# A two-layer GELU block on one core: w1's first four tiles in two transfers, and no half dummies around the transposes

## The chip, the core and the metric

The kernel runs on one core of a Trainium2 chip. The metric is the device time of one execution in microseconds, as the median of several runs. A profile of one execution stands beside it; its "span" goes from the first to the last instruction of the core, and the device time of the same execution is a little longer. In the profile PE is TensorE's matmul, PEld its weight load, DVE is VectorE, ACT ScalarE, POOL GpSimd and SP SyncE; a q behind an engine means its instruction queue.

## The reference

```python
B, S, D, F = 1, 2048, 448, 1792          # all inputs in bfloat16
def reference(x, w1, b1, w2, b2):
    h = jnp.einsum("bsd,df->bsf", x, w1) + b1
    h = _gelu(h)                          # tanh approximation
    return jnp.einsum("bsf,fd->bsd", h, w2) + b2
```

## The kernel before

The 2048 rows of x are worked through in four chunks of 512. For each chunk the first layer computes h transposed: the 1792 columns of w1 are 14 tiles ("ft") of 128, taken as seven pairs. The depth of 448 is three slices of 128 and a rest of 64. Every matmul of the layers uses half the rows of the array (64), so that two run side by side, one on the upper and one on the lower half. A pair of tiles is done in two parts, `a` (one half of the rows of each slice, three steps) and `b` (the other half, three steps and the rest of 64); `Layer1.step` picks the weights and writes down what the matmul waits for: the part of w1 that holds the tile (`w1_of`, by the list `W1CUTS`), the rest `w1r`, and the columns of x. ScalarE applies GELU and the bias b1 from PSUM (L268). The second layer multiplies by w2, VectorE adds b2 (L311), SP stores.

No scheduler decides the order. `Program` keeps one list per engine in the order in which the code appends to it, and turns each named event into a semaphore wait at the consumer. So each engine runs in exactly the order of the text, and a transfer is issued where its queue's list has it.

The opening is what the change concerns. SP issues x's first chunk (L153), then waits for ScalarE's "table" activation (L175, which loads the activation table), and only then issues the rest: w1r's first part, w1's tiles 4 to 7, w1r's second part, w1's tiles 8 to 13, w2 in two parts, b2, and the later chunks of x by transposing transfers (L147). w1's tiles 0 to 3 are issued on ScalarE's queue, right behind the table activation (`load_w1(0, "scalar")`). GpSimd makes the identity matrix, zeroes b2_z and fetches b1.

TensorE starts with dummies (`warm`, L191), matmuls of ones by ones into a PSUM tile that later work overwrites: seven of 512 columns and one of 256. `turn_all` then transposes the first chunk of x: twelve transposes of 128x128 (L338, three for each tile t = 0 to 3), whose results VectorE (t = 0, 2) and ScalarE (t = 1, 3) copy from PSUM to xT (L345), then two transposes of the rest xr (L359), which VectorE and ScalarE copy in two pieces each (L368). Then comes one more dummy of 256 columns. On VectorE's list there follow `turn_b1`, four small transposes (L180) and a cast (L182) of b1, and two copies of the odd tiles of w1r from rows 64 to 127 into rows 0 to 63 (L382). The first of them is what the last step of the first pair needs on rows 0 to 63 ("w1rU").

The first layer of chunk 0 begins with the first two pairs, `L[0]` (tiles 0 and 1) and `L[1]` (tiles 2 and 3), in halves of 256 rows of x: `L[0].a` and `L[1].a` on the first 256 rows, which need t = 0 and 1 alone, then both on the second 256. Then come `L[0].b`, `L[2].a` (tiles 4 and 5), `L[1].b`, and from there on one `a` and one `b` by turns.

Of the kernel before, what the change touches and what calls it, by code (L numbers as in the profile page):

```python
# [73 lines left out]
def bass_standalone__dense_activation_gelu__prompt_kernel(  # L74
# [13 lines left out]
    HC = SC // 2  # L88
# [9 lines left out]
    with ExitStack() as es:  # L98
# [21 lines left out]
        ones_m = one.broadcast_to([P, SC])  # L120


        W1CUTS = (0, 4, 8, 14)

        def w1_of(ft):
            return max(i for i, c in enumerate(W1CUTS) if c <= ft)

        def load_w1(i, engine="sync"):
            c0, c1 = W1CUTS[i] * P, W1CUTS[i + 1] * P
            pr.dma(engine, lambda e: e.dma_start(  # L130
                w1_sb[:, :, c0:c1], w1[0:D3, c0:c1].rearrange("(k p) f -> p k f", p=P)), ("w1", i))
# [3 lines left out]
        def load_w1r(i, engine="sync"):  # L135
            cs = slice(RCUTS[i] * P, RCUTS[i + 1] * P)
            pr.dma(engine, lambda e: e.dma_start(w1r[H:P, cs], w1[D3:D, cs]), ("w1r", i))

        def load_w2(a, b):
            pr.dma("sync", lambda e: e.dma_start(  # L140
                w2_sb[:, a:b, :], w2[a * P:b * P, :].rearrange("(f p) d -> p f d", p=P)), ("w2", a))
# [11 lines left out]
        pr.dma("sync", lambda e: e.dma_start(xn[:, :, :], x0v), "x")  # L153
        pr.barrier("sync", ["table"])
        load_w1r(0)
        load_w1(1)
        load_w1r(1)
        load_w1(2)
        load_w2(0, 7)
        load_w2(7, 14)  # L160
        pr.dma("sync", lambda e: e.dma_start(b2_bc[:, :], b2.partition_broadcast(P)), "b2")
# [12 lines left out]
               after=["b1z"])  # L174
        pr.op("scalar", lambda e: e.activation(junk[:, :], one, ACT.Gelu_apprx_tanh), event="table")  # L175
        load_w1(0, "scalar")

        def turn_b1():
            for q in range(4):
                pr.op("vector", lambda e, q=q: e.transpose(  # L180
                    b1t[32 * q:32 * q + 32, :], b1n[:, 32 * q:32 * q + 32]), after=["b1n"], event=("b1t", q))
            pr.op("vector", lambda e: e.tensor_copy(b1_f[:, :], b1t[:, 0:NFT]),  # L182
                  after=[("b1t", q) for q in range(4)], event="b1")
# [5 lines left out]
        def warm(n, cols=SC):  # L189
            for _ in range(n):  # L190
                pr.op("tensor", lambda e: e.matmul(unit[0][:, 0, 0:cols], lhsT=ones_w, rhs=ones_m[:, 0:cols],  # L191
                                                   start=True, stop=True))
# [156 lines left out]
        def turn_all():  # L349


            pr.op("vector", lambda e: e.tensor_copy(  # L352
                xr[:, :, :].rearrange("p q (two h) -> p q two h", two=2),
                xn[:, :, D3:D].rearrange("p (q two) h -> p q two h", two=2)), after=["x"], event="xr_in")
            for t in range(STC):
                turn(t)
                evac(("vector", "scalar")[t % 2], t)
            for q in range(STC // 2):
                pr.op("tensor", lambda e, q=q: e.transpose(  # L359
                    stage(0)[:, q * P:(q + 1) * P], xr[:, q, :], ident[:, :]),  # L360
                    after=["xr_in", ("xT0", 0)], event=("xr", q))
            halves = (slice(0, H), slice(H, P))
            for src, engine in enumerate(("vector", "scalar")):
                i = stage(0)[halves[src], 0:2 * P].rearrange("p (q s) -> p q s", q=2)
                for dst in (src, 1 - src):
                    o = xT[halves[dst], KT, 0:SC].rearrange("p (q two s) -> p q two s", q=2, two=2)[:, :, src, :]
                    pr.op(engine, lambda e, o=o, i=i, engine=engine:
                          e.copy(o, i) if engine == "scalar" else e.tensor_copy(o, i),  # L368
                          after=[("xr", 0), ("xr", 1)], event=("xR0", dst, src))
            busy[(3, 0)] = ("xR0", 1, 0)  # L370
            busy[(3, 2)] = ("xR0", 0, 1)

        warm(NWARM)
        warm(1, HC)
        turn_all()
        warm(1, HC)
        turn_b1()

        for i in (0, 1):
# [78 lines left out]
```

## Time and profile before

| what | value |
|---|---|
| device time, median of 5 runs | 94.38 us (94.03 to 94.87) |
| device time of the profiled execution | 94.03 us |
| its span | 92.7 us |
| PE busy | 89.7 us, 97% of the span |
| ACT busy | 38.4 us, 41% |
| DVE busy | 13.4 us, 14% |
| PE, dummies (L191) | 9 instructions, 3.6 us busy |
| PE, transposes (L338, L359) | 12 from 4.04 us and 2 from 5.03 us |
| PE, first matmul of the layers (L216) | 5.34 us after the span's start |
| x, first chunk: 448 KB on SP's queue | 3.2 us from issue to landing |
| w1, tiles 0 to 3: 384 KB on ACT's queue | 4.4 us from issue to landing |

Busy times may overlap, since a matmul that is streaming and one that drains both count. Idle time on an engine that isn't the bound costs nothing; a wait is charged to the thing that came last before the waiting engine went on.

### The profile page before, as it was taken

The page shows a single profiled execution, that of the slowest core. Times are in us where ns is not written, and L with a number is a line of the kernel's source. Part 1 is how long each engine was busy: PE and PEld are TensorE (multiplying, and loading weights), DVE is VectorE, ACT ScalarE, POOL GpSimd, SP SyncE. Part 2 cuts the span into 40 slices and gives each one's busy share as a digit, 9 for nine tenths or more (in the row PEclk, how much of TensorE's full clock was granted, in tenths as well). Part 3 has the DMA queues.
Part 4 walks back from the last instruction along what each step waited for, and adds up shares of the span by engine and source line. Part 5 has one row for each costly group of instructions (what it writes and reads, how often), then busy time and mean ns, then how long its engine had stood idle before and what let it go on. Part 6 is the DMA issues. An engine that isn't in the chain of part 4 may idle for free.

```text
span 92.7 us, 2060 instructions
## 1 busy us (share of the span) xinstructions
PE 89.7 (97%) x932; PEld 50.1 (54%) x932; DVE 13.4 (14%) x33; ACT 38.4 (41%) x63; POOL 1.7 (2%) x8
## 2 busy tenths in 40 slices
PE   6999999999999999999999999999999999999990
PEld 2474444665654444556654444565554444576990
DVE  0183001010441000000433000000333000000421
ACT  6065878600005787700003787900002887900001
POOL 6000000000000000000000000000000000000000
PEclk9999999999999999999999999999999999999999
DMA  2999999654658000000033000000022000000022
GB/s 40 358 277 298 361 324 151 111 99 99 77 96 212 21 0 7 0 0 0 0 103 102 0 0 4 0 7 0 0 99 99 0 0 7 0 0 7 33 66 99
DMA packets 12344, 7.32 MB, mean 79 GB/s; under 512 B 6960, under 2 KB 12144, under 8 KB 12336
## 3 DMA queue, kind: packets, MB, share of 16 engines
q1 hardware_dynamic: 11904, 6.80, 31.5%
q10 hardware_dynamic: 400, 0.39, 1.2%
q8 instruction: 7, 0.11, 0.5%
q0 software_dynamic: 32, 0.00, 0.0%
q14 instruction: 1, 0.01, 0.0%
HBM read 3.79 MB, written 1.84 MB: 61 GB/s over the span
## 4 chain that ended last, share of the span: by engine, by line
PE 97%; ACT 0%; issue 0%
PE u L216 92%; PE u L191 4%; PE u L338 1%; ACT out_sb L328 0%; PE u L359 0%
## 5 line engine op out<-in xcount | busy, mean ns | idle before, releaser
L268 ACT ACTIVATE g<-u,b_f 128x512 bf16<-128x512 f32 x56 | 35.0, 684 | 40.0 <-PE u L216 40.0
L216 PE MATMUL u<-w_sb,g 64*128 64x448 bf16 (+1 forms) x504 | 43.9, 328 | 0.0
L216 PE MATMUL u<-xT,w_sb 64*128 64x512 bf16 (+1 forms) x348 | 42.9, 369 | 0.0
L216 PEld LDWEIGHTS u<-w_sb,g 64*128 64x128 bf16 x504 | 28.1, 94 | 14.7
L216 PEld LDWEIGHTS u<-xT,w_sb 64*128 64x128 bf16 x348 | 19.7, 94 | 18.6 <-DMA w_sb<-in_w_dram 0.2
L311 DVE TENSOR_TENSOR out_sb<-u,b_bc 128x448 bf16<-128x448 f32 x14 | 8.1, 620 | 59.8 <-PE u L216 59.8
L216 PE MATMUL u<-xT,w1r 64*128 64x512 bf16 x56 | 16.4, 376 | 0.0
L216 PEld LDWEIGHTS u<-xT,w1r 64*128 64x128 bf16 x56 | 5.3, 94 | 3.6 <-DVE w1r L382 0.4
L191 PE MATMUL u<-const-bfloat16-1.0 128*128 128x512 bf16 (+1 forms) x9 | 3.6, 565 | 0.8 <-PEq L443 0.8
L328 ACT CAST out_sb<-u 128x224 bf16<-128x224 f32 x1 | 0.3, 345 | 9.3 <-PE u L216 9.3
L191 PEld LDWEIGHTS u<-const-bfloat16-1.0 128*128 128x128 bf16 x9 | 1.1, 135 | 2.4 <-issue 2.4
L345 ACT COPY xT<-u 128x384 bf16<-128x384 bf16 x2 | 0.9, 482 | 2.5 <-PE u L338 2.5
L175 ACT ACT_TABLE_LOAD x1 | 1.3, 1283 | 0.7 <-PEq L443 0.7
L186 DVE COPY xT<-xT 64x512 bf16<-64x512 bf16 x3 | 0.9, 289 | 3.6 <-DMA xT<-in_x_dram 3.6
L406 DVE COPY b_z<-b_bc 1x448 bf16<-1x448 bf16 x1 | 0.3, 269 | 6.7 <-DMA b_bc<-in_b_dram 6.7
L338 PEld LDWEIGHTS u<-ident,xn 128*128 128x128 bf16 x12 | 0.8, 108 | 0.6 <-issue 0.6
L338 PE MATMUL u<-ident,xn 128*128 128x128 bf16 x12 | 0.9, 236 | 0.0
L319 DVE TENSOR_TENSOR out_sb<-u,b_bc 128x448 bf16<-128x448 f32 x1 | 0.6, 625 | 1.8 <-PE u L216 1.8
L180 DVE STREAM_TRANSPOSE b1t<-b1n 32x32 bf16<-32x32 bf16 x4 | 0.8, 202 | 0.1
L368 ACT COPY xT<-u 64x256 bf16<-64x256 bf16 x2 | 0.7, 368 | 0.0
L345 DVE COPY xT<-u 128x384 bf16<-128x384 bf16 x2 | 0.7, 358 | 0.4 <-PE u L338 0.4
L352 DVE COPY xr<-xn 128x256 bf16<-128x256 bf16 x1 | 0.2, 228 | 3.0 <-DMA xn<-in_x_dram 3.0
(18 smaller groups left out, 4.8 us busy)
## 6 DMA issues: line engine op xcount, KB each, us to landing
out_dram<-out_sb SPq DMA_DIRECT2D x16, 112.0 KB, 1.7
w_sb<-in_w_dram SPq DMA_DIRECT2D x2, 784.0 KB, 8.5
w_sb<-in_w_dram SPq DMA_DIRECT2D x1, 576.0 KB, 6.3
xn<-in_x_dram SPq DMA_DIRECT2D x1, 448.0 KB, 3.2
w_sb<-in_w_dram ACTq DMA_DIRECT2D x1, 384.0 KB, 4.4
w_sb<-in_w_dram SPq DMA_DIRECT2D x1, 384.0 KB, 4.4
xT<-in_x_dram SPq DMA_TRANSPOSE x12, 4.4
w1r<-in_w_dram SPq DMA_DIRECT2D x1, 160.0 KB, 4.3
```

The lines of the kernel that those rows point to most:

```text
L175: pr.op("scalar", lambda e: e.activation(junk[:, :], one, ACT.Gelu_apprx_tanh), event="table")
L180: pr.op("vector", lambda e, q=q: e.transpose(b1t[32 * q:32 * q + 32, :], b1n[:, 32 * q:32 * q + 32]), after=["b1n"], event=("b1t", q))
L186: pr.op("vector", lambda e: e.tensor_copy(xT[0:H, KT, s0:s1], xT[H:P, KT, s0:s1]), after=after, event=event)
L191: pr.op("tensor", lambda e: e.matmul(unit[0][:, 0, 0:cols], lhsT=ones_w, rhs=ones_m[:, 0:cols], start=True, stop=True))
L216: o = pr.op("tensor", lambda e: e.matmul(unit[u][:, lo, cols], lhsT=lhsT, rhs=rhs, start=start, stop=stop, skip_group_check=skip), after=a ...
L268: pr.op("scalar", lambda e, lo=lo, ft=ft: e.activation(g[:, ft, c * SC:(c + 1) * SC], unit[u][:, lo, :], ACT.Gelu_apprx_tanh, bias=b1_f[:, ...
L311: pr.op("vector", lambda e, lo=lo, j=j: e.tensor_tensor(out=out_sb[:, j, :], in0=unit[u][:, lo, 0:D], in1=b2_bc[:, :], op=ALU.add), after= ...
L319: pr.op("vector", lambda e: e.tensor_tensor(out=out_sb[:, j, :].rearrange("p (two h) -> p two h", two=2), in0=unit[u][:, :, 0:DH], in1=b2_ ...
L328: pr.op("scalar", lambda e: e.copy(out_sb[:, j, DH:D], unit[u][:, 1, 0:DH]), after=[y[1]], event=("o", j, 1))
L338: pr.op("tensor", lambda e, k=k: e.transpose(stage(t)[:, k * P:(k + 1) * P], xn[:, t, k * P:(k + 1) * P], ident[:, :]), after=["ident", "x ...
L345: pr.op(engine, lambda e: e.copy(o, i) if engine == "scalar" else e.tensor_copy(o, i), after=[("xt", t)], event=("xT0", t))
L368: e.copy(o, i) if engine == "scalar" else e.tensor_copy(o, i),
```

## The change

`W1CUTS` gets one more cut, so that w1's tiles 0 and 1 and its tiles 2 and 3 are two transfers with a semaphore each (192 KB each, runs of 512 B instead of 1024 B). Both are issued on ScalarE's queue, one right behind the other. The numbers of SP's two parts of w1 go up by one; their contents and order stay. The half dummy before the transposes and the one after them are taken out. The order on the other engines is the same; on TensorE the first matmul of tiles 2 and 3 now has a wait of its own.

```diff
-        W1CUTS = (0, 4, 8, 14)
+        W1CUTS = (0, 2, 4, 8, 14)
...
         pr.dma("sync", lambda e: e.dma_start(xn[:, :, :], x0v), "x")
         pr.barrier("sync", ["table"])
         load_w1r(0)
-        load_w1(1)
+        load_w1(2)
         load_w1r(1)
-        load_w1(2)
+        load_w1(3)
...
         pr.op("scalar", lambda e: e.activation(junk[:, :], one, ACT.Gelu_apprx_tanh), event="table")
         load_w1(0, "scalar")
+        load_w1(1, "scalar")
...
         warm(NWARM)
-        warm(1, HC)
         turn_all()
-        warm(1, HC)
         turn_b1()
```

## The prediction

> **What bounds the kernel now.** I read the page's shares and its chain first, then the waits of the opening, then the opening in order of time on PE and on DVE, and last the transfers.
>
> The page of the kernel before, its shares and its chain:
>
> ```profile
> PE 89.7 (97%) x932; PEld 50.1 (54%) x932; DVE 13.4 (14%) x33; ACT 38.4 (41%) x63; POOL 1.7 (2%) x8
> ...
> PE 97%; ACT 0%; issue 0%
> PE u L216 92%; PE u L191 4%; PE u L338 1%; ACT out_sb L328 0%; PE u L359 0%
> ```
>
> TensorE is the bound from end to end. The two layers (L216) are 92% of the 92.7 us span, and the change doesn't touch one of their instructions. So it can only move the moment at which the stream of L216 becomes gapless. The dummies (L191) are the 4% at the start. The waits between 3.5 and 9 us say where that moment is set (engine, line, what it waited for; us, times, longest):
>
> ```profile
> PEld u L216 <- DVE w1r L382: 0.4, 1, 0.4
> ...
> PEld u L359 <- DVE xT L345: 0.2, 1, 0.2
> PEld u L216 <- DMA w_sb<-in_w_dram: 0.2, 1, 0.2
> ```
>
> The change addresses the last of these, the wait for w1's first part. The reader should see that it isn't the last wait of the opening: L216 waits again, and longer, for the copy of w1r on VectorE. In order of time (start us, us), PE and then DVE:
>
> ```profile
> 4.04 0.95 PE L338 MATMUL u<-ident,xn 128*128 128x128 bf16 x12
> 5.03 0.27 PE L359 MATMUL u<-ident,xr 128*128 128x128 bf16 x2
> 5.14 0.27 PE L191 MATMUL u<-const-bfloat16-1.0 128*128 128x256 bf16 x1
> 5.34 2.13 PE L216 MATMUL u<-xT,w_sb 64*128 64x256 bf16 x30
> 7.32 0.64 PE L216 MATMUL u<-xT,w1r 64*128 64x512 bf16 x2
> 7.57 1.67 PE L216 MATMUL u<-xT,w_sb 64*128 64x512 bf16 x12
> ```
>
> ```profile
> 3.93 0.23 DVE L352 COPY xr<-xn 128x256 bf16<-128x256 bf16 x1 [3.01 <-DMA xn<-in_x_dram]
> 4.53 0.69 DVE L345 COPY xT<-u 128x384 bf16<-128x384 bf16 x2 [0.37 <-PE u L338]
> 5.42 0.60 DVE L368 COPY xT<-u 64x256 bf16<-64x256 bf16 x2 [0.20 <-PE u L359]
> 6.04 0.90 DVE L180 STREAM_TRANSPOSE b1t<-b1n 32x32 bf16<-32x32 bf16 x4
> 7.08 0.17 DVE L182 CAST b_f<-b1t 128x14 f32<-128x14 bf16 x1
> 7.29 0.22 DVE L382 COPY w1r<-w1r 64x256 bf16<-64x256 bf16 x1
> ```
>
> From 5.42 to 7.51 VectorE has no idle time between its instructions. Its copy at L382 ends at 7.51, and the second w1r matmul of the first pair starts at 7.56. Its partner started at 7.32, so PE loses 7.56 - 7.32 = 0.24 us there. That is the slack: PE may enter L216 up to 0.24 us later, or any amount earlier, and still be at 7.56. What sets 7.56 is the chain x lands (3.91) -> transposes -> copies of x on DVE -> turning b1 -> copy of w1r.
>
> The transfers of the opening (KB, us from issue to landing):
>
> ```profile
> q10 hardware_dynamic: 400, 0.39, 1.2%
> ...
> xn<-in_x_dram SPq DMA_DIRECT2D x1, 448.0 KB, 3.2
> w_sb<-in_w_dram ACTq DMA_DIRECT2D x1, 384.0 KB, 4.4
> w_sb<-in_w_dram SPq DMA_DIRECT2D x1, 384.0 KB, 4.4
> ```
>
> ScalarE's transfer is issued at 0.80 and lands at 0.80 + 4.4 = 5.19. Its packets (queue 10: 384 of 1024 B and 16 completions) run from 3.24 to 4.62 in the trace, beginning only as those of x end (1.77 to 3.50). By the row each takes 1.2% x 92.7 x 16 / 384 = 46 ns.
>
> **The first half dummy goes.** It is 256 columns at the slow clock: 0.21 us of array, from 3.72 to 3.93. x's semaphore completes at 3.91, and the first transpose starts its weight load at 4.01; PE's wait for x is a separate instruction at 3.94, so what remains until 4.01 is the wait's own latency. The dummy was over in time. Worth: 0 (between 0 and -0.1, the time from x's semaphore to the weight load). Afterwards PE stands idle from 3.72 to 4.04, 0.32 us instead of 0.11.
>
> **The second half dummy goes.** At 5.14 it takes 256 columns, 0.11 us at full clock. The first layer's first half needs the tiles t=0 and t=1 of x, and ScalarE's copy of t=1 ends at 5.17; PE passes that wait at 5.26. With w1 there and no dummy, the weight load comes at about 5.29 instead of 5.34: 0.05 us earlier. All of it falls into the slack at 7.56. Worth: 0.
>
> **w1's first four tiles in two transfers.** The bytes stay; runs fall from 1024 to 512 B, so there are 768 packets instead of 384, 24 per DMA engine in each transfer. The second issue takes another 0.45 us of ScalarE's queue (by the first: 0.80 to 1.25), until 1.70. Queued behind it is the copy of t=1 at 4.69, so that is hidden by 3 us; the table load and the activation that SP's barrier waits for (2.24) are dispatched before both. On SP nothing is added; only numbers of w1's parts shift.
>
> When do the halves land? No packet of 512 B from w1 is in the trace. Lower end: half the bytes take half the time, so the first half's packets end 0.69 us earlier and it lands near 4.5, the second at 5.19 as now. Upper end: a 512 B packet takes as long as one of 1024 B; then the first lands at 5.19 and the second 1.39 us later, at 6.58. The Trainium skill (page "DMA: Bandwidth & Descriptors", section "Why small descriptors are slow (HBM only)") counts a packet as its bytes over 32 plus about 3 cycles: 2 x (16 + 3) = 38 cycles where there were 35. By that, 8.6% of 1.39 us, 0.12 us: an estimate, with the second half at about 5.3. The trace's neighbours support the lower half: x's 3584 B packets took 186 ns and w1's 1024 B 46 ns, so time goes by bytes there. I take 4.5 and 5.3. The same page speaks against the split in "Rules for kernel authors" (coalesce small transfers), but 192 KB behind a full x isn't limited by start-up: its packets queue behind x in any case.
>
> Need: the first half at 5.29, satisfied. The second half at 5.29 + 0.34 (the six matmuls of the first pair took 5.34 to 5.68) = 5.63. It lands at 5.3: no stall. Even at 5.87 the 0.24 us of slack would cover it.
>
> What is late next are the transfers queued behind: w1's tiles 4 to 7 land at 2.87 + 4.4 = 7.26 and are first needed at 7.57 (0.31 us in hand), and tiles 8 to 13 land at 4.02 + 6.3 = 10.3, needed near 10.6. Both are moved by the same 0.12 us and both keep 0.2 us.
>
> Sum against the profiled execution (94.03 us, span 92.7): 0 - 0.05 covered, 0.12 of transfers covered, so 94.0. The median of the five is 94.38, and this execution is the fastest.
>
> **The clock of TensorE.** The dummies run one in 0.43 us for 512 columns and the matmuls of 512 columns in the first layer one pair in 0.22, so the dummies are at half the clock. The record of the granted clock starts at 4.33, 3.55 us after the first dummy (0.78). The Trainium skill (page "TensorE: Matmul & The Clock Gate", section "Part 1: The HAM clock gate") says that the clock rises after a busy window of about 3.4 us whose phase is free, so that it varies between executions. The row agrees with a window from 0.91 to 4.33; the rule adds that other executions get the clock later. In such an execution the transposes and both dummies are at half clock, 12 x 0.107 = 1.28 us of transposes end near 5.33, the xr ones near 5.54, and the second dummy's 0.21 us is then on PE's path, because PE rather than VectorE is late. Removing it gives back up to 0.21 us there. The five times (94.03 to 94.87) would fit such a spread, but one trace can't show it. By the row alone the sum is 0; by the rule -0.21 in late executions. I take -0.1 for the median: 94.38 - 0.1 = 94.3.
>
> **The rivals.** *Hidden, as above* (0.60): 94.3, own range 94.0 to 94.7. For it: the wait at L382 behind the wait at w1.
>
> *PE's start counts in most executions* (0.14): if the clock comes late in most of them, the dummy's 0.21 us and some of the wait for w1 are saved: 94.38 - 0.21 - 0.16 = 94.0. Against it: in the only trace PE waits for VectorE afterwards.
>
> *The clock gate misses its window* (0.15), the one on the other side. Place: the idle stretch 3.72 to 4.04, 0.32 of a 3.4 us window, 9% instead of 3%, with short gaps around the xr transposes. If the window has to be busier than that, the clock rises one window later, at 4.33 + 3.41 = 7.74. Half speed for 3.41 us costs 1.7 us of matmuls, less the 0.24 + 0.05 of slack: +1.4 us, 95.8 if every execution misses, 95.1 if half do. It decides as soon as the threshold lies above 91% busy. Against it: a gap of 0.11 us was tolerated in the trace.
>
> *Small packets are slow* (0.11): with the upper end the second half lands at 6.58, PE stalls 0.95 us at tiles 2 and 3, and what follows is moved by up to 1.39 us, so tiles 4 to 7 land at 8.65 instead of 7.26 against a need of 7.57: +1.08 us, 95.5; a third of the way, +0.2. It begins to count when the second half lands after 5.87 or tiles 4 to 7 after 7.57.
>
> **How the numbers follow.** The predicted time is 94.3. About 0.5% (0.47 us) is what a measurement of this kernel can tell from no change. Faster by more, under 93.91, needs the early-start case and luck: 0.09. Slower by more, over 94.85, is most of the clock case and most of the packet case: 0.22. The rest, 0.69, is no change. The range 93.9 to 95.1 holds the hidden case, the early start, the lighter half of both slower ones, and leaves out the full misses.
>
> **What would show it.** Right: PE's L216 starts near 5.29 with no wait on w1, and still resumes near 7.56 after the wait on L382, now longer than 0.36 us; the two ACT transfers land near 4.5 and 5.3; tiles 4 to 7 near 7.4. Wrong: the clock's record starting near 7.7, a wait on w1's second half inside the first 24 matmuls of L216, a wait for tiles 4 to 7 at 7.6, or L382 itself ending earlier than 7.5, which would mean that something moved VectorE's chain that I have left standing.

## The result, and the profile after

The changed kernel takes 94.50 us in the median of 43 runs (93.94 to 94.89); the kernel before took 94.28 us in 80 runs beside it (93.86 to 94.87). The ratio is 1.0024, with a 95% interval of 1.0013 to 1.0036: about 0.23 us slower, where 0.1 us faster was forecast. Ratios leave out executions more than 1.5% above the fastest of their kernel: below, 2 of 11 of the kernel cut by rows, 1 of 22 of the one cut by depth and 7 of 12 of the one with four transfers, and none elsewhere.

The profiled execution of the changed kernel took 94.73 us with a span of 93.4 us, 0.7 us longer than the span before. The page's chain, by engine and by line:

```profile
PE 89%; DMA 6%; ACT 1%; SPq 1%; ACTq 1%; issue 0%; DVE 0%
PE u L217 89%; DMA w_sb<-in_w_dram 6%; SPq L137 1%; ACTq L130 1%; ACT L175 1%; DVE out_sb L326 0%; ACT junk L175 0%
```

Before, the chain was PE from end to end. Now a transfer of w1 stands in it. The waits from 3 to 16 us name it (engine, line, waited for; us, times, longest):

```profile
PEld u L217 <- DMA w_sb<-in_w_dram: 0.7, 1, 0.7
PE u L217 <- DMA w_sb<-in_w_dram: 0.4, 1, 0.4
PEld u L217 <- DVE w1r L381: 0.4, 1, 0.4
```

PE and the weight load wait at the same place, so the first two rows are one stop, not two. PE in order of time (start us, us) shows where it is:

```profile
4.12 0.83 PE L339 MATMUL u<-ident,xn 128*128 128x128 bf16 x12 [0.22 <-DMA xn<-in_x_dram]
4.99 0.27 PE L360 MATMUL u<-ident,xr 128*128 128x128 bf16 x2
5.28 2.13 PE L217 MATMUL u<-xT,w_sb 64*128 64x256 bf16 x30
7.25 0.67 PE L217 MATMUL u<-xT,w1r 64*128 64x512 bf16 x2
8.33 1.04 PE L217 MATMUL u<-xT,w_sb 64*128 64x512 bf16 x8 [0.41 <-DMA w_sb<-in_w_dram]
```

The layers start at 5.28 instead of 5.34, and the pause for VectorE's copy of w1r is where it was (that copy runs from 7.25 to 7.47). But the next matmuls, those of tiles 4 and 5, start at 8.33 where they had started at 7.57. That is 0.76 us, and less the 0.06 us by which the layers start earlier it is the longer span. The transfers on the page (KB, us from issue to landing) say why:

```profile
q10 hardware_dynamic: 800, 0.39, 1.4%
...
w_sb<-in_w_dram SPq DMA_DIRECT2D x1, 576.0 KB, 6.5
xn<-in_x_dram SPq DMA_DIRECT2D x1, 448.0 KB, 3.2
w_sb<-in_w_dram ACTq DMA_DIRECT2D x2, 192.0 KB, 3.9
w_sb<-in_w_dram SPq DMA_DIRECT2D x1, 384.0 KB, 5.4
```

The row of 384 KB is w1's tiles 4 to 7. It is issued at 2.87 as before and lands after 5.4 us instead of 4.4: at 8.28, not 7.26. The two halves on ScalarE's queue land at 4.61 and 5.35, in time.

### The profile page after: what moved, and what is told of

Read it like the earlier page. It is cut to its first block, busy times and chain, and to the rows that moved or that the text cites. A ratio compares the mean times of both kernels' runs of the same rounds, so it can differ in the third digit from the quotient of the medians.

```text
span 93.4 us, 2057 instructions
## 1 busy us (share of the span) xinstructions
PE 89.7 (96%) x930; PEld 46.0 (49%) x930; DVE 13.4 (14%) x33; ACT 38.4 (41%) x63; POOL 1.7 (2%) x8
## 4 chain that ended last, share of the span: by engine, by line
PE 89%; DMA 6%; ACT 1%; SPq 1%; ACTq 1%; issue 0%; DVE 0%
PE u L217 89%; DMA w_sb<-in_w_dram 6%; SPq L137 1%; ACTq L130 1%; ACT L175 1%; DVE out_sb L326 0%; ACT junk L175 0%
## 5 line engine op out<-in xcount | busy, mean ns | idle before, releaser
L217 PE MATMUL u<-w_sb,g 64*128 64x448 bf16 (+1 forms) x504 | 43.2, 328 | 0.0
L217 PE MATMUL u<-xT,w_sb 64*128 64x512 bf16 (+1 forms) x348 | 40.9, 369 | 0.4 <-DMA w_sb<-in_w_dram 0.4
L217 PEld LDWEIGHTS u<-w_sb,g 64*128 64x128 bf16 x504 | 24.5, 94 | 18.4
L217 PEld LDWEIGHTS u<-xT,w_sb 64*128 64x128 bf16 x348 | 16.9, 94 | 19.4 <-DMA w_sb<-in_w_dram 0.7
L217 PE MATMUL u<-xT,w1r 64*128 64x512 bf16 x56 | 10.9, 376 | 0.0
L217 PEld LDWEIGHTS u<-xT,w1r 64*128 64x128 bf16 x56 | 2.8, 94 | 3.7 <-DVE w1r L381 0.4
L192 PE MATMUL u<-const-bfloat16-1.0 128*128 128x512 bf16 x7 | 3.1, 621 | 0.8 <-PEq L442 0.8
L381 DVE COPY w1r<-w1r 64x256 bf16<-64x256 bf16 (+1 forms) x2 | 0.6, 288 | 1.7 <-DMA w1r<-in_w_dram 1.7
```

What stands on the lines that cost most here:

```text
L217: o = pr.op("tensor", lambda e: e.matmul(unit[u][:, lo, cols], lhsT=lhsT, rhs=rhs, start=start, stop=stop, skip_group_check=skip), after=a ...
```

## The experiments

Theory A: the split delays the transfers behind it, and TensorE stops in front of tiles 4 to 7. Theory B, the rival: the half dummies were holding the clock or the pace of the opening, and their loss is what costs. Later, A was divided into A1 (the short runs, twice the packets) and A2 (a second transfer behind the first on ScalarE's queue). Each kernel was timed in five rounds beside the kernel before.

**The split alone** (both half dummies stay; against the changed kernel):

```diff
+        warm(1, HC)
         turn_all()
+        warm(1, HC)
```

> The split alone, both half dummies kept. Theory A (the split delays the transfers behind it, w1's tiles 4 to 7 land at 7.6 or later and TensorE stops in front of them): as slow as the changed kernel, +0.2 to +0.3 us on the kernel before, tiles 4 to 7 landing after 7.6 in the trace. Theory B (the dummies were holding the clock or the pace): no slower than before, -0.1 to 0 us, tiles 4 to 7 landing near 7.3.

Ratio 1.0023 (1.0007 to 1.0039). Tiles 4 to 7 took 5.0 us to land, at 7.87:

```profile
w_sb<-in_w_dram SPq DMA_DIRECT2D x1, 384.0 KB, 5.0
```

In this profiled execution the clock rose late (the twelve transposes take 1.44 us instead of 0.83) and TensorE only came to tile 4 at 8.60, so there was no stop to be seen in it; the time, over 22 runs, is that of the full change. A as forecast, B wrong.

**The dummies alone** (from the kernel before):

```diff
-        warm(1, HC)
         turn_all()
-        warm(1, HC)
```

> The two half dummies taken out, w1's first four tiles in one transfer as before. Theory A: -0.1 to 0 us on the kernel before; first matmul of the layers still near 5.3, held by w1's landing at 5.2. Theory B: +0.2 to +0.3 us.

Ratio 0.9989 (0.9969 to 1.0009), so not slower by more than 0.09 us. Tiles 4 to 7 landed at 2.87 + 4.1 = 7.0:

```profile
w_sb<-in_w_dram SPq DMA_DIRECT2D x1, 384.0 KB, 4.1
```

B is out.

**The need put off, in the kernel before and in the changed one:**

```diff
         L[0].b()
-        L[2].a()
         L[1].b()
+        L[2].a()
```

> The kernel before with L[1].b ahead of L[2].a, so that tiles 4 to 7 are first needed some 0.86 us later (8 matmuls of 512 columns, two side by side, 0.216 us a pair), near 8.4. If the kernel before too waits for tiles 4 to 7 in many executions (its times spread from 93.9 to 94.9), this gives -0.2 to -0.4 us and a narrower spread. If its spread comes from the phase of the clock (theory B's relative), the time stays within 0.1 us and the spread stays.

> The changed kernel with the same order, L[1].b ahead of L[2].a. Theory A: the loss disappears, the time falls to that of the kernel before in the same order, -0.2 to -0.4 us on the kernel before, and no wait for w1 over 0.1 us near 8.4. Theory B: it stays +0.2 us over the kernel before in the same order.

Kernel before: 0.9998 (0.9979 to 1.0017), with the same spread, so it isn't waiting for tiles 4 to 7 as a rule. Changed kernel: 0.9997 (0.9977 to 1.0017), so its loss is gone, though this interval and that of the changed kernel (1.0013 to 1.0036) just touch. Of my two sizes the fall of 0.2 to 0.4 us was a miss; the equality of the two was as A said. PE of the changed kernel in this order:

```profile
7.28 0.66 PE L217 MATMUL u<-xT,w1r 64*128 64x512 bf16 x2
7.56 1.03 PE L217 MATMUL u<-xT,w_sb 64*128 64x512 bf16 x6
8.22 0.59 PE L217 MATMUL u<-xT,w1r 64*128 64x512 bf16 x2
8.43 0.81 PE L217 MATMUL u<-xT,w_sb 64*128 64x512 bf16 x5
```

Tiles 4 to 7 landed at 2.87 + 4.9 = 7.8 here, as late as in the split kernels above. The matmuls at 7.56 are now those of tiles 2 and 3, and the first that needs tile 4 is at 8.43: the late landing is covered, and nothing stops.

**Two transfers cut by rows** (runs of 1024 B, 64 partitions each):

```diff
-            pr.dma(engine, lambda e: e.dma_start(
-                w1_sb[:, :, c0:c1], w1[0:D3, c0:c1].rearrange("(k p) f -> p k f", p=P)), ("w1", i))
+            for r in ((0, H), (H, P)) if i == 0 else ((0, P),):
+                pr.dma(engine, lambda e, r=r: e.dma_start(
+                    w1_sb[r[0]:r[1], :, c0:c1],
+                    w1[0:D3, c0:c1].rearrange("(k p) f -> p k f", p=P)[r[0]:r[1]]), ("w1", i))
```

> The kernel before with w1's tiles 0 to 3 in two transfers on ScalarE's queue, cut by rows (64 partitions each) and not by columns: two transfers and two issues as in the change, but 384 packets of 1024 B as before. If it is the 768 short runs that delay what follows (theory A1), tiles 4 to 7 land near 7.0 and x near 3.85, and the time is that of the kernel before (within 0.1 us). If it is the second transfer on the queue (theory A2), tiles 4 to 7 land near 8.0, and it is +0.2 us.

Ratio 1.0084 (1.0049 to 1.0119). Tiles 4 to 7 landed at 2.87 + 5.7 = 8.6, with no short run in the kernel. But it doesn't test the count alone: these packets took 69 ns each instead of 46, and x landed 0.5 us later. The profiled execution took 96.87 us, well above this kernel's median of 95.37, so its landings may not be those of the others.

**Two transfers cut by depth** (runs of 1024 B, all partitions):

```diff
-            pr.dma(engine, lambda e: e.dma_start(
-                w1_sb[:, :, c0:c1], w1[0:D3, c0:c1].rearrange("(k p) f -> p k f", p=P)), ("w1", i))
+            for k0, k1 in ((0, 2), (2, KT)) if i == 0 else ((0, KT),):
+                pr.dma(engine, lambda e, k0=k0, k1=k1: e.dma_start(
+                    w1_sb[:, k0:k1, c0:c1],
+                    w1[k0 * P:k1 * P, c0:c1].rearrange("(k p) f -> p k f", p=P)), ("w1", i))
```

> The kernel before with w1's tiles 0 to 3 in two transfers on ScalarE's queue cut by depth: slices 0 and 1 in one, slice 2 in the other. Both go to all 128 partitions in runs of 1024 B, so the 384 packets are those of the kernel before, and only the second transfer is new (the row halves had slower packets besides, 69 ns instead of 46). Theory A1 (short runs): tiles 4 to 7 land near 7.0, time within 0.1 us. Theory A2 (a second transfer behind the first on this queue): they land near 8.0, and the time is +0.2 us.

The clean form of the last one: the same 384 packets as before at 47 ns, only in two transfers (256 and 128 KB). Tiles 4 to 7 landed at 2.87 + 4.6 = 7.4, between what A1 and A2 said, and tiles 8 to 13 at 4.02 + 7.2 = 11.2 (before: 10.3). In this execution TensorE started on those 0.66 us after the matmul before them, where two pairs usually start 0.22 us apart:

```profile
11.22 0.60 PE L218 MATMUL u<-xT,w_sb 64*128 64x512 bf16 x4 [0.28 <-DMA w_sb<-in_w_dram]
```

Ratio 1.0008 (0.9991 to 1.0026): a loss isn't shown, and one of 0.2 us isn't excluded. So a second transfer alone makes the rest late in the one trace, but this run doesn't settle how much of the change's delay it accounts for.

**A spare transfer of 8 KB behind w1's first part:**

```diff
+        spare = sb("spare", [P, 32], BF16)
...
         load_w1(0, "scalar")
+        pr.dma("scalar", lambda e: e.dma_start(spare[:, :], w1[0:P, 0:32]), "spare")
...
-        pr.barrier("sync", ["out"])
+        pr.barrier("sync", ["out", "spare"])
```

> The kernel before with a spare transfer of 8 KB (128 runs of 64 B, read by nobody) on ScalarE's queue right behind w1's first part: a second issue with next to no bytes. If the second issue by itself delays what follows: tiles 4 to 7 near 8.0, +0.2 us. If it takes bytes or packets in some number: they land near 7.0 to 7.2, within 0.1 us.

Landing at 2.87 + 4.1 = 7.0, ratio 0.9996 (0.9977 to 1.0015). The second issue by itself delays nothing here; a transfer of some size must come with it.

**The second half on SP's queue, behind x:**

```diff
         pr.dma("sync", lambda e: e.dma_start(xn[:, :, :], x0v), "x")
+        load_w1(1)
         pr.barrier("sync", ["table"])
...
         load_w1(0, "scalar")
-        load_w1(1, "scalar")
```

(against the split alone; both half dummies are kept)

> The split by columns with both half dummies kept, but the second half issued on SP's queue right behind x, ahead of SP's wait for the table: 768 packets of 512 B, one transfer on ScalarE's queue. Theory A1: tiles 4 to 7 near 8.0, +0.2 us. Theory A2: they land near 7.0, within 0.1 us. x itself may land later in both, since the second half then stands directly behind it.

The transfers on its page, queue 10 being ScalarE's:

```profile
q10 hardware_dynamic: 400, 0.20, 0.7%
...
w_sb<-in_w_dram SPq DMA_DIRECT2D x1, 576.0 KB, 6.1
...
w_sb<-in_w_dram SPq DMA_DIRECT2D x1, 384.0 KB, 4.2
w_sb<-in_w_dram ACTq DMA_DIRECT2D x1, 192.0 KB, 3.7
w_sb<-in_w_dram SPq DMA_DIRECT2D x1, 192.0 KB, 4.2
```

w1's first four tiles come in the same 768 short runs, and tiles 4 to 7 land after 4.2 us, at 7.0, like in the kernels with one transfer. Ratio 1.0005 (0.9989 to 1.0020). So the short runs by themselves don't bring the delay, and A1 as it was put is out; it matters where the second transfer stands. That rests on the landing, in one execution: the intervals of the times, this one and that of the split alone (1.0007 to 1.0039), overlap. Whether short runs add to the delay when both halves stand on ScalarE's queue isn't shown: cut by depth, in long runs, two transfers there gave a landing of 7.4, where halves by columns gave 7.5 to 8.3.

**Four transfers of one tile** (runs of 256 B, dummies kept):

```diff
-        W1CUTS = (0, 2, 4, 8, 14)
+        W1CUTS = (0, 1, 2, 3, 4, 8, 14)
...
-        load_w1(0, "scalar")
-        load_w1(1, "scalar")
+        for i in range(4):
+            load_w1(i, "scalar")
```

> The suspected cost taken twice more: w1's first four tiles in four transfers of one tile, 1536 packets of 256 B, dummies kept. The split in two moved the landing of tiles 4 to 7 from about 7.0 to about 8.0 us. Theory A1 (the count of packets): +384 packets cost 1.0 us, so +1152 cost about 3, landing near 10, and the time rises by 1.5 to 2.5 us. Theory A2 (the count of transfers): the three further ones cost 3 x 1.0, the same; if only bytes and the 3 cycles of a packet counted, landing near 7.4 and at most +0.2 us.

Ratio 1.0111 (1.0063 to 1.0158), and 97.12 us in the median of all runs. Tiles 4 to 7 landed at 2.87 + 5.6 = 8.5, not near 10: the delay doesn't grow in proportion to packets or transfers. Here the stops came earlier, at the third and fourth tiles themselves, which landed at 6.22 and 7.10.

**VectorE's copy of w1r ahead of the turning of b1**, and with it the best version (also the need put off and no half dummies):

```diff
-        turn_b1()
...
         for i in (0, 1):
+            if i == 1:
+                turn_b1()
```

> The kernel before with VectorE's first copy of w1r ahead of the turning of b1, so that the copy ends near 6.3 instead of 7.5. It tests the slack of 0.24 us that the prediction counted on. If that wait costs time in most executions: -0.1 to -0.24 us. If in most executions the clock rises late and TensorE is behind VectorE anyway: within 0.05 us.

> Candidate for the best version: e7's order on VectorE, L[1].b ahead of L[2].a, no half dummies, w1's first tiles in one transfer. If each of the three small gains holds where its stage is late: -0.1 to -0.4 us on the kernel before. If they are hidden behind the phase of the clock: within 0.1 us.

The copy alone: 0.9992 (0.9969 to 1.0014), that is -0.08 us with an interval of -0.29 to +0.13, which decides between neither of the two forecasts. All three: 94.13 us against 94.38 beside it, 0.9975 (0.9958 to 0.9992). This version is faster than the kernel before by about 0.24 us; which of the three carries it wasn't taken apart, and it wasn't timed beside the changed kernel.

**The changed kernel again:**

> The changed kernel once more, for a second profile of it and a ratio beside the others of this call. Theory A: tiles 4 to 7 land between 7.8 and 8.3 again; if the clock rises early, TensorE stops in front of them for 0.2 to 0.8 us, and if it rises late, it arrives after them and there is no stop. Ratio 1.002 to 1.003.

Ratio 1.0013 (0.9995 to 1.0032). Tiles 4 to 7 landed at 2.87 + 4.7 = 7.5, earlier than I expected, though still later than in any kernel with one such transfer (7.26 at most). In this execution the clock rose late:

```profile
4.07 1.44 PE L339 MATMUL u<-ident,xn 128*128 128x128 bf16 x12
5.30 0.42 PE L360 MATMUL u<-ident,xr 128*128 128x128 bf16 x2
5.65 2.60 PE L217 MATMUL u<-xT,w_sb 64*128 64x256 bf16 x30
8.08 0.38 PE L217 MATMUL u<-xT,w1r 64*128 64x512 bf16 x2
8.30 1.03 PE L217 MATMUL u<-xT,w_sb 64*128 64x512 bf16 x8
```

The twelve transposes take 1.44 us where the other profile of the same kernel has 0.83, and TensorE reaches tile 4 at 8.30, long after its landing. No stop is left. So of the two profiles of this kernel, the late landing costs time in the one whose clock rose early, and not in this one.

## Why the prediction was wrong, step by step

The landings of tiles 4 to 7 in all profiles, one execution each, as their traces have them (issued at 2.86 or 2.87):

| w1's tiles 0 to 3 | landing, us |
|---|---|
| one transfer on ScalarE's queue (kernel before, dummies alone, need put off, copy first, best version) | 7.26, 6.99, 6.72, 7.20, 6.95 |
| one, and 8 KB spare | 7.00 |
| halves on two queues | 7.01 |
| two on ScalarE's queue, by columns (changed kernel twice, split alone, need put off) | 8.28, 7.54, 7.87, 7.81 |
| two, by depth | 7.42 |
| two, by rows; four, by columns | 8.55; 8.48 |

**What failed: the step "what is late next".** It moved tiles 4 to 7 by "the same 0.12 us" and let them "keep 0.2 us". They moved from 7.02 to 7.88 in the mean of the first and the fourth row, 0.85 us, and the 0.31 us in hand was gone: the wait for tiles 4 to 7 near 7.6 that the prediction had named as a sign of being wrong. I had priced the split by the length of its packets and taken the sum of bytes and packets for the only thing that the next transfers could feel. The packets did stay cheap: by queue 10's row, 1.4% x 93.4 x 16 / 768 = 27 ns each, against 46 ns for twice the bytes, which is 17% more for a byte where the estimate had 8.6%. The term that I had put at nothing is what a second large transfer on ScalarE's queue does to the followers on SP's queue beyond its bytes and packets.

The measured 94.50 us lies inside the forecast's range of 93.9 to 95.1, but that is luck: the range reached so far up for a clock that misses its window and for slow packets, and neither came. The sign was wrong.

**What the split does there** can be seen in half-microsecond stretches. The last two columns are the share of the DMA engines that was busy and GB/s; first the kernel before, then the changed one.

```profile
5.00:5.50 0.50, 0.47 (x7) 0.33 (x9) 0.30 (x2) 0.50 (x2) 0.00 (x0) 1.00 0.99 350
5.50:6.00 0.50, 0.50 (x12) 0.45 (x10) 0.47 (x2) 0.45 (x3) 0.00 (x0) 1.00 1.15 403
```

```profile
5.00:5.50 0.50, 0.49 (x7) 0.34 (x9) 0.30 (x2) 0.50 (x2) 0.00 (x0) 1.00 0.77 252
5.50:6.00 0.50, 0.50 (x14) 0.50 (x10) 0.45 (x2) 0.45 (x3) 0.00 (x0) 1.00 1.00 324
```

From 5.0 to 6.0 the changed kernel moves 0.09 MB less ((350 + 403 - 252 - 324) x 0.5 us), at a lower share of busy DMA engines. The 448 packets of 1024 B on SP's queue that carry tiles 4 to 7 and w1r's first part take 46 ns each in the median in both, but half of them are done at 5.54 instead of 5.32, and the last ends at 7.39 instead of 6.24. And the 16 parts of tiles 4 to 7 drift apart: the first is complete at 6.3 in both, the last at 8.28 instead of 7.26. Why some parts fall behind isn't shown; the runs show that a second transfer of some size on ScalarE's queue brings it, that one of 8 KB doesn't, and that on SP's queue it doesn't. The Trainium skill (page "DMA: Bandwidth & Descriptors", section "Issuing engines are not separate DMA queues") says that transfers run on the same DMA engines whichever engine issued them, and interleave there. That fits a transfer on ScalarE's queue that slows one on SP's; that its second half costs the follower 0.85 us there, and nothing when it stands on SP's queue, is more than the page says.

**The size.** The stop was 0.76 us in the one profile that shows it, but the mean loss is 0.23 us. The runs have the shape that this needs: of the 80 runs before, 27 took under 94.1 us, of the 43 after 3. The lower quartile rose from 94.03 to 94.39, the upper from 94.47 to 94.66, and 19 runs of 20 lie at or under 94.76 in both. It is the quick executions that lose most. That they are those with the early clock is inferred from the profiles. Where there was no stop, spans are 92.6 to 92.7 with transposes of 0.83 to 0.95 us, and 93.1 to 93.7 with about 1.45; and where such a trace has a record of the granted clock, it begins at 3.63 to 4.33 in the first group and at 5.95 in the second. The timed runs have no such record.

A part of the loss may have another path, which the prediction also put at nothing: x itself landed at 3.93 to 4.18 with two halves by columns on ScalarE's queue and at 3.82 to 3.92 with one transfer, 0.16 us later in the mean, and the transposes wait for x. With a late clock nothing hides that. No run separates it from the stop at tiles 4 to 7; the order that puts their need off brought back the whole loss within its interval.

**What held.** The layers start at 5.28 (forecast 5.29). The halves land at 4.61 and 5.35 (4.5 and 5.3). The second w1r matmul is at 7.53 (7.56): the start gained fell into the slack, and the wait on w1 was worth nothing. The dummies cost nothing to remove: 0.9989 for them alone, -0.10 us with an interval of -0.29 to +0.08, where -0.1 was forecast. In late-clock executions the first matmul of the layers comes at 5.58 to 5.65 without them and at 5.78 to 5.79 with them in the kernels with one transfer, so some 0.16 us of the 0.21 counted.

**What was mis-sized beside it.** The wait at L382 was read as 0.24 us, from one w1r matmul to the other. From the first w1r matmul to the last matmul of the program it is 82.97 us in the profile before and 82.81 us in that of the copy first, where both start at once, so the wait costs 0.16 us with the early clock. In the median, taking it away alone gave -0.08 us, which can't be told from zero.

**The rivals.** "Small packets are slow" had the right place (tiles 4 to 7 after 7.57) and a landing too late (8.65, measured 7.54 and 8.28), for a wrong cause: the second half landed at 5.35, not 6.58. That its "a third of the way, +0.2" is the measured loss is chance. "The clock gate misses its window" isn't seen in the changed kernel: its slowest of 43 runs took 94.89 us, the slowest before 94.87, and in its profile the clock was up from the first transpose at 4.12 (twelve in 0.83 us), though TensorE had stood idle before it (0.22 us by the bracket).

## What to carry to other kernels

A wait that ends first isn't a wait worth removing: look for the next wait behind it, and measure the slack. When a transfer is cut in two, follow the transfers that run after it on every queue to their first users, and write down how many tenths of a microsecond each has in hand; here 0.31 us was all that stood between a harmless edit and a stop. If a second half is needed early, try it on the queue of its followers, ahead of them: here it delayed them by nothing there, and by 0.85 us from the other queue.

## What the runs showed that was not expected

The phase of the clock goes with most of the spread of these times, 93.9 to 94.9 us: of the profiled executions without a stop, those with an early clock took 93.9 to 94.0 us, those with a late one 94.4 to 95.0. It also decides what the opening waits for: with the early clock TensorE waits for VectorE's copy and for transfers, with the late one these waits are 0.3 us at most.

In the kernel cut by rows, x came late and TensorE stood idle for 0.45 us before the transposes:

```profile
4.59 1.44 PE L340 MATMUL u<-ident,xn 128*128 128x128 bf16 x12 [0.45 <-DMA xn<-in_x_dram]
...
6.60 3.81 PE L218 MATMUL u<-xT,w_sb 64*128 64x256 bf16 x30
```

The thirty matmuls that begin the layers take 3.81 us there and 2.13 in the changed kernel, and the trace's record of the granted clock begins at 10.07, where the other traces that have one begin at 3.63 to 5.95. So a much later clock does occur, at the price of 1.7 us that the prediction had put on it; this is one execution, of 96.87 us, and whether the idle stretch brought it isn't shown. And in this trace transfers to 64 partitions ran at 69 ns for 1024 B where those to 128 took 46.
